# Turning q and k of one block and x of two blocks by transposing DMA instead of on TensorE

## The chip, the cores and the metric

The kernel runs on one core of a Trainium2 chip. The metric is the device time of one execution in microseconds (us). Three runs of the kernel before took 304.11, 304.75 and 304.83 us, so the median is 304.75 us. A profiled execution gives the trace that the text reads.

## The reference

Attention with a sliding window and a linear bias on the distance comes first, then a normalised two-layer network with a residual. B = 8 batches, H = 8 heads, S = 576 tokens, D = 64 per head, so 512 features per token and 2048 hidden ones.

```python
rel = pos[:, None] - pos[None, :]
bias = slopes[:, None, None] * (-np.abs(rel))            # one slope per head
mask = (rel >= 0) & (rel < 128)
scores = np.where(mask, q @ k^T / sqrt(D) + bias, -1e9)  # per batch and head
attn = softmax(scores)
x = heads of (attn @ v) side by side                     # B x 576 x 512
xn = (x - mean) / sqrt(var + 1e-6) * g_ln
out = x + relu(xn @ w_ch1) @ w_ch2                       # 512 -> 2048 -> 512
```

Inputs and output are float32; the kernel works on float16 tiles with float32 sums.

## The kernel before

**Blocks.** Two batches make a pair `p` (0 to 3). The tokens of a pair are cut into nine blocks of 128 rows: `blk` 0 to 7 are 128 tokens of one batch each (even ones of the first batch, odd ones of the second), and `blk` 8 (`T`) holds the last 64 tokens of both batches. All 36 blocks have a number n = 9 p + blk; "block 13" in the text is n = 13. Blocks are gathered in twelve groups for the network: groups 0 to 5 have two blocks each (group 3 has blocks 6 and 7), groups 6 to 11 have four.

**Loading.** `load_qk` and `load_v` issue DMAs on GpSimd's queue, which turn float32 into float16 on the way. q and k come for two blocks at once (index `i` = blk // 2; `i` = 4 is block 8 alone) and in two DMAs each, one for each batch. For `by_dma(p, i)` false, two neighbouring tokens go to one partition, so that one row of a DMA is 128 numbers (512 bytes of float32); for true, the tokens lie in their natural order and a row is 64 numbers (256 bytes). A GpSimd DMA waits, among other things, until the one eight before it has landed.

**Turning q and k.** The scores need q and k with the head's features on the partitions. `turn(p, i)` does that. Where `by_dma` is false, `transposed` makes transposes of 64x64 on TensorE (line 304), two times 16 for block 8, and copies take them out of PSUM on VectorE and ScalarE (line 348). Where it is true, `dma_start_transpose` is issued on SyncE's queue (line 322), one DMA for q and one for k and for each batch. `BY_DMA_TURN = (1, 0)` sets the border: pair 0 (blocks 0 to 8) is turned on TensorE, and everything from block 9 on by DMA.

**Turning x.** A block's attention output is `x`; the first network product needs it centred and with the features on the partitions, in the group's tile `xT`. For blocks below `BY_DMA` (8), `centre` writes the centred `xc` and `turn_x` makes four transposes on TensorE (line 638) and one copy out of PSUM (line 639). From block 8 on `normal` issues a transposing DMA on SyncE (line 548), but for the three blocks in `BY_PE`.

**Order.** `steps` is a list written out by hand, of scores, masks, values, turns and decays for blocks 4 to 9, and made by a loop from block 8 on. The main program runs the network's products (`mlp1`, line 815, the first product; `mlp2`, line 889, the second) and `weave_at` puts the next steps behind those products whose numbers it is given. TensorE, SyncE and GpSimd run in exactly the order in which the program issues. The scores are made by `attend` (line 442); the values by line 496. The scores of block n + 2 stand behind the values of block n.

SyncE's queue carries the stores of the results too (line 1052): two for each of the first blocks, each waiting until VectorE has made the result. A DMA on SyncE also waits until the one eight before it has landed. Raw q and k tiles and their turned forms have four buffers each, `xT` three, `xc` three.

Of the kernel before, what the change touches and what calls it, by code (L numbers as in the profile page):

```python
# [17 lines left out]
P = 128  # L18
# [8 lines left out]
FAST, HURRIED, DEFERRED, SETTLED, TURNED = 6, 11, 14, 15, 18  # L27

NV = 10
BY_DMA_TURN = (1, 0)  # L30
AHEAD, HELD = 8, (19, 23)

FIRST_GROUPS, FIRST = 2, 4
# [27 lines left out]
def kernel(  # L61
# [10 lines left out]
    nc = tc.nc  # L72
# [140 lines left out]
    def by_dma(p, i):  # L213
        return (p, i) >= BY_DMA_TURN

# [31 lines left out]
    order = [(p, blk) for p in range(NPAIR) for blk in range(NSLOT)]  # L247
# [137 lines left out]
    def psum(name, banks=None):  # L385


        if not ring:
            return ps_mm.tile([P, DM], FP32, tag="mm", name=name)
        t = (banks or ring)[0]  # L390
        if banks is None:
            ring.append(ring.pop(0))
        return t
# [127 lines left out]
    turned_x = {}  # L521

    centred = {}
# [33 lines left out]
    def inverse_roots(n=None):  # L557

        for left, m in roots[:]:
            if left <= 0 or m == n:  # L560
                roots.remove([left, m])
                inverse_root(m)
# [66 lines left out]
    def turn_x(g, at, p, blk, copy):  # L629
# [8 lines left out]
            nc.tensor.transpose(ps[:, kb, :], xc[:, kb * P : (kb + 1) * P], iden)  # L638
        copy(out=xT[:, :, at * P : (at + 1) * P], in_=ps)

    def variance(n):
        st = small.tile([P, nc.vector.BN_STATS_DIM], FP32, tag="st", name="st")
        nc.vector.bn_stats(out=st, in_=xs[order[n]])  # L643
        nc.vector.bn_aggr(out=moments[:, n, :], in_=st)
# [31 lines left out]
    members, home = [], {}  # L676
    for g, size in enumerate(GROUPS):
        n = sum(GROUPS[:g])
# [5 lines left out]
    def turn_step(n, *how):  # L684
        p, blk = order[n]
        return [(turn, p, blk // 2) + how]

    def scores_step(n):
        return [(scores,) + order[n]]

    def load_step(n):
        if n in HELD or n + AHEAD > count:
            return []
        if n < HELD[0]:
            return [(load_until, place[n + AHEAD])]
        return [(hold_loads, n), (load_until, place[min(n + AHEAD - 1, count - 1)])]
# [6 lines left out]
    def values_steps(n):  # L703
        p, blk = order[n]
        return [
            [(masks, p, blk), (values, p, blk, 0)],
            [(values, p, blk, 1), (centre, p, blk)] + load_step(n) * (n < BY_DMA),
        ]

    def x_step(n, copy=nc.vector.tensor_copy):  # L710
        return [(turn_x,) + home[n] + order[n] + (copy,)] if n < BY_DMA else []

    def variance_of(n):

        return [(variance, n)] + [(inv_std, n - 3, 4)] * (n % 4 == 3)

    def masks_of(n, *halves):
        return [(masks,) + order[n] + halves]

    def warm_step(n):  # L720
        return [[(warm, n)]]
# [8 lines left out]
    steps = warm_step(11) + [[(turn_first,)]] + warm_step(3)  # L730
# [17 lines left out]
    steps += [x_step(4) + masks_of(5)]  # L748
    steps += [values_steps(5)[0], turn_step(6, True), values_steps(5)[1]]
    steps += [scores_step(6) + [(decay, m_tail, 4)]]  # L750
    steps += [x_step(5) + masks_of(6) + turn_step(9), scores_step(7) + variance_of(4), values_steps(6)[0]]

    steps += [values_steps(6)[1], masks_of(7), x_step(6, nc.scalar.copy), variance_of(5)]
    steps += [*values_steps(7), x_step(7) + variance_of(6)]
    low, high = ([(decay, m_late, 5, range(h, h + 4))] for h in (0, 4))
    steps += [turn_step(8) + low + variance_of(7), scores_step(8) + turn_step(11)]
    steps += [[(scores_tail, 0)] + scores_step(9) + high + masks_of(8)]


# [38 lines left out]
    def advance_to(n):  # L798
        nonlocal done
        while done < min(n, len(steps)):  # L800
            for f, *args in steps[done]:
                f(*args)
            done += 1
# [4 lines left out]
    def hidden_tile(g):  # L808
        hidden[g] = hidden_pool.tile([P, NFB, 4 * P], FP16, tag="ht", name="ht")

    def ch1(g, fb, ps, cols):

        w = w1 if g < FIRST_GROUPS else w1g
        for kb in range(NKB):
            nc.tensor.matmul(  # L815
                ps[:, cols],
                w[:, kb, fb * P : (fb + 1) * P],
                turned_x[g][:, kb, cols],
                start=(kb == 0),
                stop=(kb == NKB - 1),  # L820
            )

    def relu(g, fb, ps, on_dve):
        cols = slice(0, len(members[g]) * P)
        out, ps = hidden[g][:, fb, cols], ps[:, cols]
        if on_dve:
            nc.vector.tensor_scalar(
                out=out, in0=ps, scalar1=0.0, scalar2=None, op0=ALU.max
            )
        else:  # L830
            nc.scalar.activation(out=out, in_=ps, func=AF.Relu)  # L831
# [35 lines left out]
    def mlp1(g, on_dve=()):  # L867
        cols = slice(0, len(members[g]) * P)
        hidden_tile(g)
        turn_about = chain(*zip(range(QF), range(QF, NFB)))  # L870
        for u, fb in enumerate(turn_about if g >= FAST else range(NFB)):
            ps = psum("ps_m1")
            ch1(g, fb, ps, cols)
            relu(g, fb, ps, u in on_dve)
            yield cols
            if g >= FAST and u == 10:
                for i in range(4):
                    combine_hidden(g, 0, i)

    def mlp2(g, parts=((0, NFB),)):  # L880

        ht = hidden[g]
        sums = {}
        for first, end in parts:
            for at, (p, blk) in enumerate(members[g]):
                if first == 0:
                    sums[at] = ps_mm.tile([P, DM], FP32, tag="mm", name="ps_m2")
                for fb in range(first, end):
                    nc.tensor.matmul(  # L889
                        sums[at],  # L890
                        ht[:, fb, at * P : (at + 1) * P],
                        w2[:, fb, :],
                        start=(fb == 0),
                        stop=(fb == NFB - 1),
                    )
                    if fb % 4 == 3 and fb < NFB - 1:
                        yield DM
                if end == NFB:
                    finish(p, blk, sums[at])
                    yield DM  # L900
# [10 lines left out]
    def combine_hidden(g, part, i):  # L911


        f = slice(part * QF // 2, (part + 1) * QF // 2)
        s1, s2, s3, s4 = (hidden_sum(g, j) for j in range(4))
        a11, a12 = (hidden_quarter(g, 0, j) for j in range(2))
        a21, a22 = (hidden_quarter(g, 1, j) for j in range(2))
        dst, a, b, op = (
            (s1, a21, a22, ALU.add),
            (s2, s1, a11, ALU.subtract),  # L920
            (s4, a12, s2, ALU.subtract),
            (s3, a11, a21, ALU.subtract),
        )[i]
        nc.vector.tensor_tensor(out=dst[:, f], in0=a[:, f], in1=b[:, f], op=op)
# [131 lines left out]
    def weave_at(units, *places, also=(), late=0):  # L1056
        nonlocal hold
        hold = late
        for u, _ in enumerate(units):
            for root in roots:  # L1060
                root[0] -= 1
            inverse_roots()
            advance_to(done + places.count(u))
            if u in also:
                next(combined, None)
# [12 lines left out]
    with tc.manual_schedule(engines={engine.PE, engine.SP, engine.Pool}):  # L1078
        with tc.manual_schedule(engines={engine.Activation, engine.DVE}):
            advance_to(first)  # L1080
            weave_at(mlp1_first(), 2, 3, 4, 8, 10, 12, 17, 24, 30, 34)
            weave_at(mlp2(0, [(fb, fb + 4) for fb in range(0, NFB, 4)]), 0, 1, 3, 4, 4, 5)
            weave_at(mlp2(1), 0, 1, 2, 3, 4, 6, 6)
            weave_at(mlp1(2), 0, 3, 5, 5, 6, 8, 13)
            weave_at(mlp2(2), 0, 2, 4, 6, 7)


            weave_at(mlp1(3, (9, 10, 11)), 8, 8, 12, 15, late=3)
            weave_at(mlp2(3), 0, 1, 1, 3, 4, 4, 6, 6)
            weave_at(mlp1(4, (11,)), 0, 4, 8, 10, 11, 14, also=(2, 12), late=3)  # L1090
            weave_at(mlp2(4), 0, 2, 2, 5, 5, 7, also=(1,))
            weave_at(mlp1(5, (0, 7)), 0, 4, 6, 8, 10, also=(3, 7, 11), late=3)
            weave_at(mlp2(5), 0, 1, 2, 4, 6, 7)
            ring += [ps_mm.tile([P, DM], FP32, tag="mm", name="ps_r") for _ in range(4)]
            for g in range(6, len(GROUPS)):
                weave_at(
                    mlp1(g), 0, 2, 5, 7, 8, 10, 13, 15, also=(1, 4) if g == 6 else ()
                )
                weave_at(fast_mlp2(g), 1, 3, 6, 7, 7, 10, 12, 13)
# [31 lines left out]
```

## Time and profile before

| | |
|---|---|
| median of 3 runs | 304.75 us |
| the profiled execution | 304.07 us |
| its span (first to last instruction) | 302.3 us |
| TensorE busy | 295.8 us, 98% of the span |
| VectorE busy | 216.8 us, 72% |
| ScalarE busy | 181.3 us, 60% |
| loads on GpSimd's queue (q0) | 108688 packets, 18.65 MB |
| DMAs on SyncE's queue (q1) | 49090 packets, 19.45 MB |
| granted TensorE clock | 0.994 |

The profiled execution's own time is 1.8 us more than its span. In the lines shown further down, PE is TensorE, DVE VectorE, ACT ScalarE, POOL GpSimd and SP SyncE; a q behind the name means the engine's queue, which issues and waits. L638 is line 638 of the kernel. The chain is the work that ended last, followed back from the last instruction. A busy share of DMA packets can be over 100%, since each of the 16 DMA engines has several packets under way at once.

### The profile page before, as it was taken

Reading aid. Unit: us, or ns where it says so; the run is one execution under the profiler, and the core shown is the slowest. Engines: PE = TensorE matmul, PEld = TensorE weight load, DVE = VectorE, ACT = ScalarE, POOL = GpSimd, SP = SyncE. Lnnn points to the kernel's source line nnn. Section 1 sums busy time; section 2 is a strip of 40 time slices with the busy share of each in tenths; the row PEclk is TensorE's granted clock in tenths of the full one; section 3 lists DMA queues with packets and bytes.
Section 4 is the critical chain, followed back from the end, with each engine's and each line's share of the span. In section 5 each row is a group of like instructions: output and inputs, shape, how many; then the busy total and the mean of one; then the engine's idle time right before and its main releaser. Section 6 shows DMA issues by size and latency. Waiting matters only on the chain.

```text
span 302.3 us, 8809 instructions
## 1 busy us (share of the span) xinstructions
PE 295.8 (98%) x3652; PEld 201.0 (66%) x3652; DVE 216.8 (72%) x518; ACT 181.3 (60%) x358; POOL 109.6 (36%) x145
## 2 busy tenths in 40 slices
PE   8999999999999999999999999999999999999994
PEld 2479755857768585557865786578657865784583
DVE  2589777867687797657976797679767976750463
ACT  5498776878769386485358536753685367306600
POOL 8936359843568333442173218312400000000001
PEclk9799999999999999999999999999999999999999
DMA  9999999999999999999899939999992051021004
GB/s 99 164 189 194 196 188 176 144 164 156 171 165 129 168 128 183 153 180 134 86 166 185 132 62 148 112 189 132 149 154 50 20 165 28 2 88 69 2 0 139
DMA packets 158042, 38.99 MB, mean 129 GB/s; under 512 B 147953, under 2 KB 153585, under 8 KB 158002
## 3 DMA queue, kind: packets, MB, share of 16 engines
q0 software_dynamic: 108688, 18.65, 88.3%
q1 hardware_dynamic: 49090, 19.45, 40.5%
q8 instruction: 28, 0.46, 0.7%
q10 hardware_dynamic: 224, 0.33, 0.3%
q14 instruction: 12, 0.10, 0.2%
HBM read 36.97 MB, written 9.44 MB: 154 GB/s over the span
## 4 chain that ended last, share of the span: by engine, by line
PE 95%; DMA 2%; DVE 1%; POOL 1%; issue 0%; DVEq 0%; POOLq 0%
PE ps_r L815 28%; PE ps_r L955 24%; PE ps_m L815 14%; PE ps_m L889 14%; PE ps_sc L442 6%; PE ps_r L496 3%; PE ps_pv L496 2%; DMA k<-in_k_dram 2%; PE ps_warm L286 1%; PE ps_tx L638 1%; DVE o L973 1%; PE ps_tr L304 1%; PE ps_sc L580 1%; POOL q L231 1%; PE ps_sc L304 0%; PE ps_sc L286 0%
## 5 line engine op out<-in xcount | busy, mean ns | idle before, releaser
L815 PEld LDWEIGHTS <-w1g 128*128 128x128 f16 x640 | 61.2, 98 | 47.1 <-issue 0.2
L815 PE MATMUL ps_r<-xT,w1g 128*128 128x512 f16 x384 | 84.8, 379 | 0.0
L451 ACT ACTIVATE probs<-ps_sc 128x1024 f16<-128x1024 f32 x56 | 54.2, 1025 | 35.4 <-PE ps_sc L442 35.4
L831 ACT ACTIVATE ht<-ps_r 128x512 f16<-128x512 f32 x96 | 55.7, 595 | 23.8 <-PE ps_r L815 23.8
L889 PE MATMUL ps_m<-w,ht 128*128 128x512 f16 x192 | 45.3, 380 | 0.0
L955 PE MATMUL ps_r<-w,ht 128*128 128x256 f16 x384 | 43.9, 273 | 0.0
L241 POOL DMA_DIRECT2D vx<-in_v_dram x40 | 34.0, 858 | 19.5 <-DMA k<-in_k_dram 3.9
L955 PEld LDWEIGHTS <-ht 128*128 128x128 f16 x384 | 37.2, 98 | 4.7
L831 ACT ACTIVATE ht<-ps_m 128x256 f16<-128x256 f32 x86 | 30.8, 391 | 5.3 <-PE ps_m L815 3.2
L228 POOL DMA_DIRECT2D k<-in_k_dram x30 | 25.3, 854 | 16.6 <-DMA q<-in_q_dram 14.0
L1048 POOL DMA_DIRECT2D out_dram<-o x2 | 1.1, 560 | 82.1 <-DVE o L973 82.1
L228 POOL DMA_DIRECT2D q<-in_q_dram x30 | 25.4, 853 | 14.9 <-DMA vx<-in_v_dram 13.8
L815 PE MATMUL ps_m<-xT,w1g 128*128 128x256 f16 x256 | 30.0, 273 | 0.0
L889 PEld LDWEIGHTS <-ht 128*128 128x128 f16 x192 | 17.3, 98 | 18.3
L462 DVE TENSOR_TENSOR probs<-probs,m 128x1024 f16<-128x1024 f16 x44 | 27.8, 672 | 0.1
L504 DVE RECIPROCAL rec<-ps_r 128x4 f32<-128x4 f32 x36 | 6.3, 174 | 28.1 <-PE ps_r L496 28.1
L643 DVE BATCH_NORM_STATS2 st<-x 128x6 f32<-128x512 f16 x36 | 24.8, 688 | 0.7
L955 PE MATMUL ps_r<-w,hs 128*128 128x256 f16 x192 | 21.9, 273 | 0.0
L973 DVE TENSOR_TENSOR o<-ps_r,o 128x512 f32<-128x512 f32 (+1 forms) x25 | 16.5, 664 | 5.6 <-PE ps_r L955 5.1
L496 PEld LDWEIGHTS <-probs 128*128 128x128 f16 x416 | 17.4, 97 | 4.5 <-DVE probs L462 0.3
L442 PE MATMUL ps_sc<-q,k 64*64 64x128 f16 (+1 forms) x1088 | 20.0, 210 | 0.3 <-DVE k L344 0.3
L955 PEld LDWEIGHTS <-hs 128*128 128x128 f16 x192 | 18.8, 98 | 2.2
(98 smaller groups left out, 360.7 us busy)
## 6 DMA issues: line engine op xcount, KB each, us to landing
out_dram<-o SPq DMA_DIRECT2D x22, 256.0 KB, 4.1
q<-in_q_dram POOLq DMA_DIRECT2D x32, 128.0 KB, 8.8
k<-in_k_dram POOLq DMA_DIRECT2D x32, 128.0 KB, 9.7
vx<-in_v_dram POOLq DMA_DIRECT2D x32, 128.0 KB, 11.7
w<-in_moe_w_ch_dram POOLq DMA_DIRECT2D x6, 512.0 KB, 10.4
out_dram<-o SPq DMA_DIRECT2D x24, 128.0 KB, 5.5
w<-in_moe_w_ch_dram POOLq DMA_DIRECT2D x4, 256.0 KB, 11.4
q<-in_q_dram POOLq DMA_DIRECT2D x8, 64.0 KB, 8.5
```

The lines of the kernel that those rows point to most:

```text
L228: nc.gpsimd.dma_start(out=dst, in_=rows.rearrange("h p d -> p h d"))
L241: nc.gpsimd.dma_start(out=vx[p0 : p0 + n, :, 0:D], in_=v[b, :, t0 : t0 + n, :].rearrange("h p d -> p h d"),)
L442: nc.tensor.matmul(at_q, kt[rows, hp, cols], of_q, start=True, stop=True,)
L451: nc.scalar.activation(out=dst.rearrange("p (n j) q -> p j n q", j=2), in_=ps.rearrange("p j n t q -> p j n (t q)"), func=AF.Exp, scale=in ...
L462: nc.vector.tensor_tensor(out=dst, in0=dst, in1=mask, op=ALU.mult)
L496: nc.tensor.matmul(ps[:, i, :], pr[:, h, t, :], vext[(p * NSLOT + o) % NV][:, h, :], start=(n == 0), stop=(n == len(terms) - 1),)
L643: nc.vector.bn_stats(out=st, in_=xs[order[n]])
L815: nc.tensor.matmul(ps[:, cols], w[:, kb, fb * P : (fb + 1) * P], turned_x[g][:, kb, cols], start=(kb == 0), stop=(kb == NKB - 1),)
L831: nc.scalar.activation(out=out, in_=ps, func=AF.Relu)
L889: nc.tensor.matmul(sums[at], ht[:, fb, at * P : (at + 1) * P], w2[:, fb, :], start=(fb == 0), stop=(fb == NFB - 1),)
L955: nc.tensor.matmul(banks[name][pair][:, pair, :], lhs[:, fb, pair * P : (pair + 1) * P], rhs[:, fb, :], start=(first and fb == 0 and (pair ...
L973: nc.vector.tensor_tensor(out=o[:, at, cols], in0=banks[name][at.start][:, at, :], in1=(x if to_x else o)[:, at, cols], op=ALU.add,)
```

## The change

The border of `BY_DMA_TURN` moves to (0, 4), so that block 8 is loaded in its natural order and its q and k are turned by two transposing DMAs. The turn of block 8 moves ahead of the turn of blocks 9 and 10 in the steps. `send_x` is new: it issues a transposing DMA for x of blocks 6 and 7, right behind their `centre`, in place of `turn_x` on TensorE. One step fewer is left, so `weave_at` for group 2's first product has one place less. The buffers are as before. In SyncE's queue the new DMAs stand as follows: stores of blocks 0 to 2, turn of 8, turn of 9/10, store of block 3, x of 6, x of 7, turn of 11/12.

```diff
@@ -27,7 +27,7 @@
 FAST, HURRIED, DEFERRED, SETTLED, TURNED = 6, 11, 14, 15, 18
 
 NV = 10
-BY_DMA_TURN = (1, 0)
+BY_DMA_TURN = (0, 4)
 AHEAD, HELD = 8, (19, 23)
 
 FIRST_GROUPS, FIRST = 2, 4
@@ -638,6 +638,11 @@
             nc.tensor.transpose(ps[:, kb, :], xc[:, kb * P : (kb + 1) * P], iden)
         copy(out=xT[:, :, at * P : (at + 1) * P], in_=ps)
 
+    def send_x(g, at, p, blk):
+
+        xT = turned_x[g][:, :, at * P : (at + 1) * P]
+        nc.sync.dma_start_transpose(out=xT, in_=centred.pop((p, blk)))
+
     def variance(n):
         st = small.tile([P, nc.vector.BN_STATS_DIM], FP32, tag="st", name="st")
         nc.vector.bn_stats(out=st, in_=xs[order[n]])
@@ -710,6 +715,9 @@
     def x_step(n, copy=nc.vector.tensor_copy):
         return [(turn_x,) + home[n] + order[n] + (copy,)] if n < BY_DMA else []
 
+    def send_step(n):
+        return [(send_x,) + home[n] + order[n]]
+
     def variance_of(n):
 
         return [(variance, n)] + [(inv_std, n - 3, 4)] * (n % 4 == 3)
@@ -748,12 +756,12 @@
     steps += [x_step(4) + masks_of(5)]
     steps += [values_steps(5)[0], turn_step(6, True), values_steps(5)[1]]
     steps += [scores_step(6) + [(decay, m_tail, 4)]]
-    steps += [x_step(5) + masks_of(6) + turn_step(9), scores_step(7) + variance_of(4), values_steps(6)[0]]
-
-    steps += [values_steps(6)[1], masks_of(7), x_step(6, nc.scalar.copy), variance_of(5)]
-    steps += [*values_steps(7), x_step(7) + variance_of(6)]
+    steps += [x_step(5) + masks_of(6) + turn_step(8) + turn_step(9), scores_step(7) + variance_of(4), values_steps(6)[0]]
+
+    steps += [values_steps(6)[1] + send_step(6), masks_of(7), variance_of(5)]
+    steps += [values_steps(7)[0], values_steps(7)[1] + send_step(7), variance_of(6)]
     low, high = ([(decay, m_late, 5, range(h, h + 4))] for h in (0, 4))
-    steps += [turn_step(8) + low + variance_of(7), scores_step(8) + turn_step(11)]
+    steps += [low + variance_of(7), scores_step(8) + turn_step(11)]
     steps += [[(scores_tail, 0)] + scores_step(9) + high + masks_of(8)]
 
 
@@ -1081,7 +1089,7 @@
             weave_at(mlp1_first(), 2, 3, 4, 8, 10, 12, 17, 24, 30, 34)
             weave_at(mlp2(0, [(fb, fb + 4) for fb in range(0, NFB, 4)]), 0, 1, 3, 4, 4, 5)
             weave_at(mlp2(1), 0, 1, 2, 3, 4, 6, 6)
-            weave_at(mlp1(2), 0, 3, 5, 5, 6, 8, 13)
+            weave_at(mlp1(2), 0, 3, 5, 6, 8, 13)
             weave_at(mlp2(2), 0, 2, 4, 6, 7)
```

## The prediction

> **What bounds the kernel now.** First the head of the page and its chain: TensorE works for nearly the whole span, and the chain that ended last is TensorE's own.
>
> ```profile
> span 302.3 us, 8809 instructions
> PE 295.8 (98%) x3652; PEld 201.0 (66%) x3652; DVE 216.8 (72%) x518; ACT 181.3 (60%) x358; POOL 109.6 (36%) x145
> ...
> PE 95%; DMA 2%; DVE 1%; POOL 1%; issue 0%; DVEq 0%; POOLq 0%
> ```
>
> So TensorE time taken out is time won, as long as nothing that TensorE needs comes late. Next the chain in order of time (start, duration, what) around the three turns that the change touches.
>
> ```profile
> 50.74 1.73 PE ps_m L889 x8
> ...
> 57.11 0.22 PE ps_tx L638 x4
> ...
> 61.31 0.22 PE ps_tx L638 x4
> ...
> 63.27 0.62 PE ps_tr L304 x32
> 63.90 1.83 PE ps_m L889 x8
> ...
> 72.27 7.09 PE ps_m L815 x64
> ```
>
> 57.11 and 61.31 turn x of blocks 6 and 7, 63.27 turns q and k of block 8, and 72.27 is the first product of group 3, which reads the turned x of 6 and 7. No idle time stands between the pieces. Third, SyncE's queue over the same time (start, duration, what), since the turns go there.
>
> ```profile
> 50.13 1.11 SPq L1052 DMA_DIRECT2D out_dram<-o  x2
> 52.58 2.69 SPq L322 DMA_TRANSPOSE q<-q  x2
> 55.44 2.68 SPq L322 DMA_TRANSPOSE k<-k  x2
> 58.22 2.31 SPq L1052 DMA_DIRECT2D out_dram<-o  x2
> 61.11 2.62 SPq L322 DMA_TRANSPOSE q<-q  x2
> 64.10 3.26 SPq L322 DMA_TRANSPOSE k<-k  x2
> ...
> 76.37 3.33 SPq L322 DMA_TRANSPOSE k<-k  x2
> ```
>
> These are the turns of block pairs 9/10 (52.58), 11/12 (61.11) and, last line, 13/14. One transposing DMA holds the queue for some 1.34 us. In the DMA view of narrow stretches the issues at 64.10 and 76.37 land after:
>
> ```profile
> k<-k SPq DMA_TRANSPOSE x1, 9.0
> k<-k SPq DMA_TRANSPOSE x1, 7.9
> ```
>
> Last, what transposes do to the loads. The DMA view of 75.3 to 76.3 us, in which no transpose moves, and then of 66.5 to 69.5 us, in which they do; q0 carries GpSimd's loads, q1 SyncE's DMAs (packets, MB, share):
>
> ```profile
> q0 software_dynamic: 1195, 0.15, 236.4%
> q1 hardware_dynamic: 9, 0.01, 2.5%
> ```
> ```profile
> q0 software_dynamic: 1525, 0.19, 98.3%
> q1 hardware_dynamic: 1139, 0.28, 71.8%
> ```
>
> Alone, the loads run at 1195 packets a us; beside transposes at 508, with 380 transposing packets. And the rate from 55 to 73.3 us, in 40 slices of 0.46 us, in which eight transposes ran:
>
> ```profile
> GB/s 166 173 170 90 43 126 153 187 142 151 66 14 10 156 153 153 159 152 151 158 158 256 315 198 155 158 160 150 159 160 147 190 149 81 8 53 154 155 151 155
> ```
>
> Three times (slices of 43, of 14 and 10, and of 8) all queues all but stop, for 1.0 to 1.5 us. From 35 to 50 us, without transposes, no slice is under 108. So this stretch of DMA is full, though TensorE does not yet wait for it.
>
> **What goes.** On TensorE 8 + 32 transposes and nothing else: its order is otherwise the same. From the chain: 0.22 + 0.22 + 0.62, and the eight products after the turn of block 8 take 1.83 us instead of 1.73, so 0.10 more: 1.16 us, all on the path. The four copies out of PSUM (0.42 and 0.73 us on VectorE, 0.58 and 0.73 on ScalarE) go too; I count them at nothing, as both engines wait for TensorE there. Four PSUM tiles less can only free waits, of which the chain shows none. That alone is 304.07 - 1.16 = 302.91 us against the profiled execution, which lies 0.68 us under the median of 304.75; so 303.6 as a median.
>
> **What comes.** Four transposing DMAs in SyncE's queue: q and k of block 8 ahead of turn 9/10, x of 6 and 7 behind the store of block 3 and ahead of turn 11/12. And the four loads of block 8 fetch rows of 256 bytes instead of 512: by the code 512 packets each instead of 256. GpSimd takes 0.68 us instead of 0.58 to issue one (rows of the same form later on): 0.4 us in all, covered, as GpSimd then waits until 45.31 for another reason.
>
> *Block 8.* Its loads are issued by 43.8 and land 5.3 to 6.3 us later, by 50.1 at the latest, so its two transposes can go at 51.3, once the stores of block 2 are out. Landing 9.0 us after issue, k is there at 61.6; scores of block 8 stand at 65.7 - 1.06 = 64.6. Covered by 3 us. Behind them turn 9/10 issues about 1.5 us later than now: its first k lands at about 66, and its scores stand at 67.9 - 1.16 = 66.7. Covered, but only just.
>
> *x of 6 and 7.* The centred x is ready (60.5 for block 7). On the queue: 51.3 + 6 x 1.34 + 1.1 for two stores = 60.5 for x6, 61.9 for x7. Needed: 72.2 - 1.16 = 71.0. If the issue sets the pace, x7 lands 7.3 to 9.0 us later (the neighbouring rows), at 69.2 to 70.9: in time. If the transposing queue sets the pace, x7 is the eighth of a row of eight transposes with two stores among them, as the second k of 11/12 is now: issued at 66.1 and, with the 9.0 us of the k before it (its own landing is not recorded), there at about 75.1. The row begins 1.3 us sooner, so 73.8: 2.8 us late. The queue looks full in the 66.5 row, so I take the middle, 0.9 us late; ends 0 and 2.8.
>
> *Loads behind them.* Each added transpose has 512 packets, 1.35 us at 380 a us, in which the loads lose (1195 - 508) x 1.35 = 925 packets or 0.77 us; four make 3.1. The added load packets are 1024, at most 0.9 us; I take 0.6, as their neighbours land in 5 to 6 us and the queue was not yet full. Three stops for eight transposes make one and a half for four; I take one of 1.1 us (ends 0 and 1.8). Together the loads of block pair 13/14 land 4.8 us later (3.1 to 5.8). Nothing shortens that on the way: GpSimd waits for landed DMAs before it issues more (14.0 and 13.8 us of such waits at its k and q loads). Turn 13/14 starts now when its loads land; its first k, issued at 76.37, lands at 84.3 and is used by the scores of block 13 at 87.9. Slack 3.7, less the 1.16 that TensorE comes sooner: 2.5. So 4.8 makes TensorE wait 2.3 us (0.6 to 3.3). What it waited for x7 counts within this, since it moves the scores back too. What is late next would be turn 15/16 (first k landing at 96.3 for scores at 100.6, 4.3 us of slack, and 2.3 more after the wait): covered.
>
> Sum: -1.16 + 2.3 = +1.14 us, 304.07 + 1.14 = 305.2 for the profiled execution, 305.9 as a median.
>
> **A rule against this change.** The trace turns a 128x512 tile on TensorE in 0.22 us and by DMA in 7.3 to 9.0 us here. The Trainium skill, "VectorE: DVE Perf Modes", section "The three transpose paths" (and its rules for authors), prefers TensorE wherever PSUM will do as a destination, with 390 ns for one 128x128 turn there against 1309 ns by DMA. The direction agrees; the size does not, as four turns in 0.22 us are 55 ns apart. By the page's 390 ns, as an estimate, the eight turns of x alone would free 3.1 us instead of 0.44, and the sum would be a gain of 1.5 us.
>
> **Rivals.**
> *All lands in time.* The issue paces x7, and the transposes mostly use slots that the loads leave. For it: the 7.3 us rows, and 3.7 us of slack at 13. Between 146 and 152 us, with no loads, a transpose lands in 2.4 us and its 512 packets take about 0.64 us (1993 packets, 41.9% of 6 us). Were that the whole cost, four would be 2.6 us, 0.1 over the slack before stops. Against it: the halved load rate. It decides as long as x7 lands by 71.0 and the loads of 13/14 come less than 2.5 us later. Time: 303.6, not slower but 1.16 us faster. The Trainium skill, "Advanced Engine Details and Errata", section "X-Bar Transpose (TRN2)", has transposes as fast as plain DMAs at 350 to 400 GB/s, an estimate of 0.35 us for one; that would also lead here, but the slices above show 150 to 160 GB/s.
> *Only x7 is late,* and the loads recover by 73 us. TensorE waits 0.3 to 2 us at the start of group 3's first product: 303.9 to 305.6, middle 304.7.
> *Worse than forecast.* Two or more added stops, or turn 9/10 late as well: waits of 3.5 to 5 us, 307.1 to 308.6. For it: three stops in one row of eight. Against it: the loads run without stops from 75 to 79 us, and turn 15/16 has its slack.
> *The change doesn't do what it says:* TensorE's order shows the transposes gone, so this is out.
>
> **Numbers.** Forecast (turn 13/14 late) 0.42; all in time 0.30; x7 alone 0.21; worse 0.07. The forecast's own range is 304.2 to 306.9, from 0.6 and 3.3 us of waiting. The range from 303.4 (the in-time case, with 0.2 for scatter) to 307.2 leaves out some 0.1 to 0.2. About 0.3%, 0.9 us, is what a measurement can tell from no change: faster by more is the in-time case, 0.30; the x7 case and the low end of the forecast lie within, 0.23; slower 0.47.
>
> **What would show it.** Right: TensorE's chain has gaps released by DMA near 71 us (group 3's first product) and near 87 us (scores of block 13), with 1 to 3 us between them; the loads of 13/14 land about 5 us later; outside, the pieces of the chain keep their lengths. Wrong: no such gaps and a span 1.1 us shorter; or a first gap at the scores of block 9, or lateness that is still there after 110 us.

## The result, and the profile after

The changed kernel takes 307.02 us (median of 8 runs, 305.26 to 309.39) against 304.37 us (median of 8 runs, 303.01 to 304.83): a ratio of 1.0095, 95% interval 1.0072 to 1.0118. It is 2.65 us slower, where 1.14 us were forecast. The profiled execution took 306.27 us. The ratios here and below leave out runs that took over 1.5% more than the fastest of their kernel.

First the head of the page and its chain by engine, for the kernel after.

```profile
span 304.5 us, 8738 instructions
PE 295.5 (97%) x3612; PEld 200.3 (66%) x3612; DVE 215.9 (71%) x516; ACT 180.6 (59%) x356; POOL 110.2 (36%) x145
...
PE 89%; DMA 4%; DVE 3%; issue 1%; POOL 1%; SPq 1%; ACT 1%; DVEq 0%; POOLq 0%
```

The 40 transposes are gone (3612 matrix instructions instead of 3652), and yet TensorE is busy for 295.5 us instead of 295.8. So something else has become longer on it. The chain's share of TensorE fell from 95% to 89%: it now leaves TensorE somewhere. Where, the chain in order of time tells (start, duration, what):

```profile
64.41 8.61 DMA xT<-xc
73.02 0.05 issue
73.07 8.83 PE ps_m L823 x64
...
90.54 0.47 PE ps_sc L442 x16
```

The transposing DMA of x of block 7 is issued at 64.41 and lands at 73.02; group 3's first product starts the moment it does. Two things are new. TensorE waited: its view of waits has one long entry.

```profile
PE ps_m L823 <- DMA xT<-xc: 2.5, 1, 2.5
...
PE ps_sc L442 <- DMA k<-k: 0.4, 1, 0.4
```

And the product itself is longer: its 64 instructions took 7.09 us before and take 8.83 us now. Tables of single microseconds show why (columns: stretch and its length, busy time and count of PE, PEld, DVE, ACT and POOL, granted clock, DMA share, GB/s):

```profile
72.00:73.00 1.00, 0.00 (x0) 0.00 (x0) 0.97 (x4) 0.00 (x0) 0.00 (x0) 1.00 1.23 123
73.00:74.00 1.00, 0.93 (x5) 0.71 (x6) 0.54 (x1) 0.00 (x0) 0.14 (x1) 0.59 1.81 155
74.00:75.00 1.00, 1.00 (x7) 0.73 (x5) 0.00 (x0) 0.47 (x2) 0.74 (x1) 0.50 1.89 153
75.00:76.00 1.00, 1.00 (x7) 0.69 (x6) 0.00 (x0) 0.53 (x2) 0.00 (x0) 0.50 1.99 153
76.00:77.00 1.00, 1.00 (x8) 0.78 (x7) 0.00 (x0) 0.53 (x2) 0.70 (x1) 0.70 1.66 155
77.00:78.00 1.00, 1.00 (x11) 0.90 (x10) 0.00 (x0) 0.77 (x3) 0.47 (x2) 1.00 1.61 154
```

The third figure from the end is the granted clock. It is still 1.00 while TensorE stands idle, falls to half when work starts again, and is back at 1.00 by 77. In the records the half clock lasts 3.41 us, in which 16 products come 213 ns apart instead of 109 ns: 16 x 104 ns = 1.7 us. The lateness of one transfer therefore cost twice, 2.46 us of waiting and 1.74 us of slow work behind it.

The Trainium skill, "TensorE: Matmul & The Clock Gate", has the clock fall back after about 3 us without work (section "Why this matters for your kernels") and states the limit as some 3.4 us (section "HAM oscillation — how this bites in real kernels"). The trace does not agree with that limit: 2.46 us were enough here.

SyncE's queue (start, duration, what) shows how x came to be that late:

```profile
50.87 1.35 SPq L322 DMA_TRANSPOSE q<-q  x1
52.40 1.29 SPq L322 DMA_TRANSPOSE k<-k  x1
53.85 2.87 SPq L322 DMA_TRANSPOSE q<-q  x2
56.89 4.71 SPq L322 DMA_TRANSPOSE k<-k  x2
61.71 1.21 SPq L1060 DMA_DIRECT2D out_dram<-o  x2
63.02 2.65 SPq L644 DMA_TRANSPOSE xT<-xc  x2
65.83 3.24 SPq L322 DMA_TRANSPOSE q<-q  x2
69.23 3.57 SPq L322 DMA_TRANSPOSE k<-k  x2
```

50.87 and 52.40 are q and k of block 8, and the turn of 9/10 follows 1.3 to 1.5 us later than before. But the two k of 9/10 hold the queue for 4.71 us instead of 2.68, and x7 (x of block 7; x6 is that of block 6) goes out at 64.41, not at 61.9 as worked out. The rates from 55 to 73.3 us, in 40 slices of 0.46 us, show something else in both places:

```profile
GB/s 141 142 117 137 154 100 144 88 9 9 73 151 145 129 136 147 159 140 152 153 151 155 154 156 143 153 256 256 254 156 160 150 155 193 142 102 8 56 159 150
```

All queues stop twice. The slices of 9 (58.7 to 59.6 us) lie within the 4.71 us for which the two k hold the queue, and the slice of 8 (71.5 to 71.9 us) within the 8.61 us for which x7 is under way. So about 1 us at the issue and somewhat less in flight go with stops, which the prediction had counted for the loads alone. How late x7 would have been without them is not shown.

DMA is as full as before; the DMA view of 66.5 to 69.5 us (packets, MB, share):

```profile
q0 software_dynamic: 1654, 0.21, 107.8%
q1 hardware_dynamic: 716, 0.40, 63.6%
```

In the same stretch SyncE's DMAs moved 1139 packets and 0.28 MB before. The 716 packets are fewer but have more bytes, since stores of results, in larger packets, are among them; so the two counts can't be compared as a rate of transposing. What the prediction expected at 87 us is not there: the first k of block 13 lands at 87.08, and its scores stand at 90.54. Its loads, as far as their landing is recorded, land 2.6 to 4.2 us later than before, but TensorE is later too.

How the profiled executions add up: ahead of the first removed turn, the changed kernel's chain is already 1.08 us sooner (49.66 for 50.74, the same eight products); nothing in the change does that, and the kernel of the first experiment, the same up to there, has 50.85. So -1.08 of scatter, -1.16 for the turns, +0.4 at the scores of block 9, +2.46 and +1.74 at group 3: +2.36, against +2.2 in the spans.

### The profile page after: what moved, and what is told of

The parts are those of the page before. It is cut to its first block, busy times and chain, and to the rows that moved or that the text cites. A ratio compares the mean times of both kernels' runs of the same rounds, so it can differ in the third digit from the quotient of the medians.

```text
span 304.5 us, 8738 instructions
## 1 busy us (share of the span) xinstructions
PE 295.5 (97%) x3612; PEld 200.3 (66%) x3612; DVE 215.9 (71%) x516; ACT 180.6 (59%) x356; POOL 110.2 (36%) x145
## 4 chain that ended last, share of the span: by engine, by line
PE 89%; DMA 4%; DVE 3%; issue 1%; POOL 1%; SPq 1%; ACT 1%; DVEq 0%; POOLq 0%
PE ps_r L823 28%; PE ps_r L963 24%; PE ps_m L823 13%; PE ps_m L897 11%; PE ps_sc L442 5%; DMA xT<-xc 3%; PE ps_r L496 3%; PE ps_pv L496 2%; DMA k<-in_k_dram 1%; PE ps_tx L638 1%; DVE o L981 1%; PE ps_sc L580 1%; POOL q L231 0%; PE ps_sc L304 0%; SPq L644 0%
## 5 line engine op out<-in xcount | busy, mean ns | idle before, releaser
L823 PEld LDWEIGHTS <-w1g 128*128 128x128 f16 x640 | 62.1, 99 | 50.6 <-DMA xT<-xc 2.6
L823 PE MATMUL ps_m<-xT,w1g 128*128 128x256 f16 x256 | 31.4, 282 | 2.5 <-DMA xT<-xc 2.5
L228 POOL DMA_DIRECT2D q<-in_q_dram x32 | 26.7, 839 | 19.0 <-DMA vx<-in_v_dram 16.4
L228 POOL DMA_DIRECT2D k<-in_k_dram x32 | 26.6, 838 | 14.7 <-DMA q<-in_q_dram 13.6
```

What stands on the lines that cost most here:

```text
L228: nc.gpsimd.dma_start(out=dst, in_=rows.rearrange("h p d -> p h d"))
L823: nc.tensor.matmul(ps[:, cols], w[:, kb, fb * P : (fb + 1) * P], turned_x[g][:, kb, cols], start=(kb == 0), stop=(kb == NKB - 1),)
```

## The experiments

The theories: (A) x7 comes late because the two halves of the change stand in one queue, and idle time then halves the clock; against it, that x by DMA is late by itself (B), that block 8's q and k upset the turns behind them (C), and, for what paces the queue, the loads (D) or the transposes themselves (E).

**x alone.** Turn x of 6 and 7 by DMA, keep block 8 on TensorE in its old place. Against the kernel after:

```diff
-BY_DMA_TURN = (0, 4)
+BY_DMA_TURN = (1, 0)
-    steps += [x_step(5) + masks_of(6) + turn_step(8) + turn_step(9), scores_step(7) + variance_of(4), values_steps(6)[0]]
+    steps += [x_step(5) + masks_of(6) + turn_step(9), scores_step(7) + variance_of(4), values_steps(6)[0]]
-    steps += [low + variance_of(7), scores_step(8) + turn_step(11)]
+    steps += [turn_step(8) + low + variance_of(7), scores_step(8) + turn_step(11)]
```

> x of blocks 6 and 7 turned by DMA; q and k of block 8 stay on TensorE, in their old place. Theory A (x7 is late because two transposes of block 8 stand ahead of it in the queue, and the idle time then halves the clock): x7 is the sixth of its row and not the eighth and lands about 70 us, 1.5 us or more before its product; no wait at group 3, the saving of 0.44 us is kept, about 304.0 us against 304.4. Theory B (a transposing DMA is too slow for x7 wherever it stands): a wait of 2 us or more at group 3 and a half clock behind it, 307 us.

Measured: 303.66 us, ratio 0.9984 (0.9964 to 1.0003). x7 was issued at 61.80 and landed at 69.54. The chain at group 3:

```profile
72.06 7.09 PE ps_m L823 x64
```

No wait and full clock; x7 was there 2.5 us early, so x by DMA is not late by itself: B is out. Against this kernel the change issues x7 2.61 us later, it takes 0.88 us longer (with a stop of the queues in it, where x7 here had none), and TensorE is ready 1.45 us sooner (1.19 of it the scatter named above, 49.66 for 50.85): 4.94 us, which uses up the 2.5 us and leaves the 2.46 us of waiting.

**q and k of block 8 alone.** The kernel before with that half of the change.

```diff
-BY_DMA_TURN = (1, 0)
+BY_DMA_TURN = (0, 4)
-    steps += [x_step(5) + masks_of(6) + turn_step(9), scores_step(7) + variance_of(4), values_steps(6)[0]]
+    steps += [x_step(5) + masks_of(6) + turn_step(8) + turn_step(9), scores_step(7) + variance_of(4), values_steps(6)[0]]
-    steps += [turn_step(8) + low + variance_of(7), scores_step(8) + turn_step(11)]
+    steps += [low + variance_of(7), scores_step(8) + turn_step(11)]
```

> q and k of block 8 turned by DMA ahead of 9/10; x of 6 and 7 stay on TensorE. Theory A: nothing is waited for at group 3; 0.72 us saved, less a wait of some 0.4 us at the scores of block 9: 303.9 to 304.2. Theory C (the step of the prediction: the added transposes make the loads and the turn of 13/14 late): half of the added transposes make the loads 2.7 us late against 3.0 of slack, 303.7 to 304.7, with the first wait at the scores of block 13.

Measured: 303.35 us, ratio 0.9981 (0.9957 to 1.0005). Group 3's product stands at 71.56 for 7.09 us, without a wait, and the scores of block 13 do not wait either, so nothing of C is seen here. Each half alone is no slower than before; the medians are 0.47 and 0.78 us under that of the kernel before in the same runs, together 1.25, close to the 1.16 us counted. Both at once should then have won 1.25 and lost 2.65: 3.9 us, give or take about 1 us by the three intervals, come of the two meeting.

**A filler in the idle time.** The kernel after, with twelve products on constants where TensorE would wait for x7.

```diff
             weave_at(mlp2(2), 0, 2, 4, 6, 7)
+            warm(12)
```

> The changed kernel with twelve idle products of 128x512 (2.6 us) on TensorE between the scores of block 10 and the first product of group 3, so that it works through the wait. Theory A: the wait for x7 ends when it did, but the clock stays at 1.0 and the 16 products at half clock go, 1.7 us: about 305.3 us against 307.0. If the slow products had another cause than the idle time, nothing is won: 307.0 or more.

Measured: 306.14 us, ratio 1.0063 (1.0037 to 1.0090). The filler in TensorE's timeline, and then lines of its chain:

```profile
71.17 2.76 PE L286 MATMUL ps_warm<-ones 128*128 128x512 f16 x12
```
```profile
65.75 8.60 DMA xT<-xc
...
74.49 7.15 PE ps_m L823 x64
```

x7 came at 74.4 in this execution, later still than in the kernel after, and TensorE waited all the same; but the products behind it ran at full clock, 7.15 us instead of 8.83. The mean granted clock of the other executions says the same. A stretch of 3.41 us at half clock in 302 us makes 0.994; seven of the eight runs of the kernel after have 0.992 to 0.994, and the eighth, at 1.0, is the fastest (305.26 us). With the filler none of twelve is below 0.997. (The kernel before has 0.996 or more in all 87 runs made beside the experiments; the 0.994 of its profiled execution was another, early stretch.) That the half clock is caused by the idle time is thereby shown. Its 1.7 us are read from the trace; the times alone do not settle them, since the two ratios' intervals overlap.

**Block 8's turn earlier.** The kernel after, with q and k of block 8 ahead of the store of block 2 in SyncE's queue.

```diff
-    steps += [values_steps(5)[0], turn_step(6, True), values_steps(5)[1]]
+    steps += [values_steps(5)[0], turn_step(6, True), values_steps(5)[1] + turn_step(8)]
-    steps += [x_step(5) + masks_of(6) + turn_step(8) + turn_step(9), scores_step(7) + variance_of(4), values_steps(6)[0]]
+    steps += [x_step(5) + masks_of(6) + turn_step(9), scores_step(7) + variance_of(4), values_steps(6)[0]]
```

> The changed kernel with the turn of block 8 ahead of the store of block 2 in SyncE's queue, where the queue sits idle until that store's result is there. All four added transposes stay. Theory A: x7 is the sixth transpose behind the store and lands at 70 us, as needed: no wait or less than 1 us, 303.2 to 304.5 us. Theory C: with x7 in time the turn of 13/14 is late instead, waits of 1 to 2.3 us at the scores of block 13 and a half clock behind: 305 to 307. Theory B: 307.

Measured: 304.45 us, ratio 1.0013 (0.9984 to 1.0043). x7 is issued at 62.92, 1.49 us sooner, and group 3 starts without a DMA wait. TensorE's timeline:

```profile
71.28 7.16 PE L823 MATMUL ps_m<-xT,w1g 128*128 128x256 f16 x64
...
87.84 0.51 PE L442 MATMUL ps_sc<-q,k 64*64 64x128 f16 x28 [0.58 <-DMA k<-k]
```

Here the forecast's own step comes out: with group 3 in time, the scores of block 13 wait for their k, for 0.58 us instead of the 2.3 worked out, and without a loss of clock. Their loads, as far as recorded, land 3.3 to 4.4 us later than in the kernel before, where the prediction had 4.8. One of twelve runs still has a clock of 0.994, and it is the slowest, 307.28 us.

**Fewer loads, first try.** The kernel after without the loads of v of blocks 10 to 16.

```diff
+        if 10 <= p * NSLOT + blk <= 16:
+            return
```

> The changed kernel without the loads of v for blocks 10 to 16 (seven loads of 128 KB less; the values of those blocks are then made from old numbers). Theory D (the transposing queue is slow because each of its packets shares the DMA engines with a packet of the loads): with fewer loads under way between 51 and 75 us a transpose moves in less than 1.3 us, x7 lands 2 us or more sooner than in the changed kernel (about 70 to 71 us), no wait at group 3, 303 to 304 us. Theory E (the queue or its issue is slow by itself, 1.3 us and more for each transpose): x7 lands at about 73 as before, the wait of some 2.5 us stays, 306 to 307 us.

Measured: 304.85 us, ratio 1.0010 (0.9976 to 1.0044). The profiled execution still waited:

```profile
72.92 8.83 PE L825 MATMUL ps_m<-xT,w1g 128*128 128x256 f16 x64 [2.41 <-DMA xT<-xc]
```

GpSimd issued its next loads into the places left free, so its queue stayed full (5829 packets of loads from 66 to 78 us, 5950 in the kernel after). The ten runs fall in two: six of 302.95 to 305.47 us with a clock of 0.998 or more, and four of 306.20 to 307.51 at 0.993 or 0.994, of which the last is not in the ratio. Something had changed for the better, but the trace can't say what, as it is of the late kind.

**The kernel after once more.** A single run, for a second trace.

> The changed kernel once more, for a second trace of the same wait. Theory A: again a wait for x7 before the first product of group 3, of 1.5 to 4 us, and half clock for some 3 us behind it; the scatter of the kernel's times comes from the length of this wait. Otherwise the wait lies elsewhere in this trace.

Measured: 307.74 us. TensorE's timeline:

```profile
74.47 8.83 PE L823 MATMUL ps_m<-xT,w1g 128*128 128x256 f16 x64 [2.54 <-DMA xT<-xc]
```

The product starts 1.4 us later than in the first trace, but the wait (2.54 us for 2.46) and the 8.83 us are as before: no accident of one trace. A rival remains. In all four traces in which x7 was late (the kernel after twice, the filler, the first try with fewer loads) a stop of all queues falls into the time for which x7 is under way; with x alone, and with block 8's turn earlier, x7 lands before the next stop. A later issue thus also let x7 run into a stop, and no run separates the two.

**Fewer loads, second try.** The kernel after with q and k of blocks 13 to 17 set to zero by GpSimd, and one head of eight of v of blocks 10 to 17 loaded.

```diff
+            if p == 1 and i > 1:
+                nc.gpsimd.memset(t, 0.0)
+                return
+        few = 1 if 10 <= p * NSLOT + blk <= 17 else H
-                out=vx[p0 : p0 + n, :, 0:D],
+                out=vx[p0 : p0 + n, 0:few, 0:D],
```

> The changed kernel with q and k of blocks 13 to 17 set to zero on GpSimd instead of loaded, and of v of blocks 10 to 17 one head of eight loaded; so the load queue is nearly empty from about 60 us, and stays so until the loads of block 18. Theory D (the transposing queue is slow because its packets share the DMA engines with the loads): from 60 us on a transpose moves in 0.9 us or less, x7 lands 3 us or more sooner after its issue than the 8.6 us of the changed kernel, so by about 69 us; no wait at group 3, full clock: 303.0 to 303.6 us. Theory E (queue or issue slow by itself): 8 us from issue to landing and the wait of 2.5 us as before, 306 to 307 us.

Measured: 303.21 us, ratio 0.9975 (0.9952 to 0.9997). Nine of the ten runs have a clock of 0.998 or more; the tenth, 307.17 us at 0.994, is not in the ratio, and no trace of it tells why. First the DMA view of 66.5 to 69.5 us, then TensorE's timeline:

```profile
q1 hardware_dynamic: 2230, 0.65, 132.2%
q0 software_dynamic: 144, 0.02, 8.9%
```
```profile
70.76 7.16 PE L827 MATMUL ps_m<-xT,w1g 128*128 128x256 f16 x64
...
87.50 0.51 PE L446 MATMUL ps_sc<-q,k 64*64 64x128 f16 x28 [0.75 <-DMA k<-k]
```

With nearly no loads beside them, SyncE's DMAs move 0.65 MB in 3 us instead of 0.40 (2230 packets instead of 716, but of another mix). x6 lands 5.47 us after its issue, not 7.30; x7 is issued at 64.57, even a little later than in the kernel after, and is there by 70.76, so at most 6.2 us instead of 8.61, though a stop falls into its flight here too. TensorE does not wait. So D holds for the flight, and E as the whole cause is out: sharing with the loads makes a transpose some 2 us slower. That is less than the 3 us that D foretold, and the issue of x7 did not come sooner. The Trainium skill, "DMA: Bandwidth & Descriptors", section "Queues, rings and completion order", has each DMA engine serve its queues in turn, packet by packet; the trace agrees, as the packets of the one queue go up when the other has few, though other ways of sharing would show the same.

The scores of block 13 wait 0.75 us although their q and k were not loaded at all. The chain has the first k of block 13:

```profile
77.68 9.77 DMA k<-k
```

It is issued at 77.68, behind stores and other turns, and takes 9.77 us to land. By then the loads of block 18 and on are under way (4140 packets of loads from 77.6 to 87.5 us, 2276 packets of SyncE's), and the queues stop once, near 80 us. So this wait does not tell the queue from the loads.

**Which half to keep.** Two more: block 8's early turn by DMA with x of 7 alone on TensorE (of 6 by DMA), and with both x on TensorE, that is, the kernel before with

```diff
-BY_DMA_TURN = (1, 0)
+BY_DMA_TURN = (0, 4)
-    steps += [values_steps(5)[0], turn_step(6, True), values_steps(5)[1]]
+    steps += [values_steps(5)[0], turn_step(6, True), values_steps(5)[1] + turn_step(8)]
-    steps += [turn_step(8) + low + variance_of(7), scores_step(8) + turn_step(11)]
+    steps += [low + variance_of(7), scores_step(8) + turn_step(11)]
```

The edit of the former, against the kernel with block 8's turn earlier:

```diff
-    steps += [values_steps(7)[0], values_steps(7)[1] + send_step(7), variance_of(6)]
+    steps += [values_steps(7)[0], values_steps(7)[1], x_step(7) + variance_of(6)]
```

> As the kernel with the early turn of block 8, but x of block 7 on TensorE; x of block 6 by DMA. Three added transposes. Saving 0.94 us. If the turn of 13/14 is late in proportion to the added transposes, it comes 0.8 us sooner than with four and its wait of 0.6 us is gone: about 303.4 us. Otherwise a wait of 0.3 to 0.6 at the scores of block 13, 303.9.

Measured: 304.76 us, ratio 1.0003 (0.9981 to 1.0025). Group 3 is in time, but TensorE waits 1.43 us for a load of v near 20 us (the kernel with block 8 alone by DMA waits 1.20 us there) and 1.36 us for k at 118 us. Why there, is open. One of the twelve runs, 308.73 us at a clock of 0.992, is not in the ratio.

> q and k of block 8 by DMA, ahead of the store of block 2; x of 6 and 7 on TensorE. If the waits are what the change lost, this keeps its 0.72 us of TensorE time and two added transposes: about 303.6 us against 304.3, no wait on a DMA after 60 us. If turn 13/14 is already late with two added transposes, a wait of up to 0.5 us at the scores of block 13 and 304.1.

Measured: 303.81 us, ratio 0.9981 (0.9961 to 1.0001); its profiled execution has no wait of TensorE for a DMA. Run again:

> The early turn of block 8 by DMA with x of 6 and 7 on TensorE, measured a second time, to tell whether it beats the kernel before: 0.72 us of TensorE time saved and no wait, 0.9976; with the first measurement (0.9981) the upper end should come under 1. If scatter in the loads eats it, 0.999 to 1.001.

Measured: 303.42 us, ratio 0.9976 (0.9954 to 0.9997). In its profiled execution TensorE waits for a DMA for 0.5 us or less at a time. This version is 0.2% faster than before, at the edge of what was measured, and by the two ratios 1.2% faster than the kernel after (0.9976 / 1.0095 = 0.988).

## Why the prediction was right or wrong, step by step

- **What goes, 1.16 us of TensorE:** right. The two halves alone bring 0.47 and 0.78 us in the medians, where 0.44 and 0.72 were counted.
- **Block 8 covered, turn 9/10 only just:** block 8 was; the scores of block 9 waited 0.4 us.
- **x of 6 and 7, "0.9 us late; ends 0 and 2.8":** this is the step that failed. The wait was 2.46 us, and it stood in the place of the one forecast at block 13. The flight (issue to landing), 8.61 us, lay within the 7.3 to 9.0. The issue was mis-sized: the sum 51.3 + 6 x 1.34 + 1.1 gave each transpose 1.34 us of the queue and nothing for delays, and the two k of 9/10 held it for 4.71 us, so that x7 went out at 64.41 instead of 61.9. A stop of all queues, about 1 us, lies in those 4.71 us; what made the rest of the 2.03 us by which they exceed the 2.68 of before stays open. The end at which the queue sets the pace gave 73.8 for x7, and it came at 73.02. The row of 66.5 us, which showed the queue full, spoke for that end, and the middle was taken.
- **What TensorE does after a wait:** the missing term, put at nothing without a reason. The sum had every product at the length it had before; 1.74 us of half clock came on top of the wait.
- **Turn 13/14 late, 2.3 us:** did not happen. The loads were 2.6 to 4.2 us later instead of 4.8 (the stop of 1.1 us taken for them was not added: two stops from 55 to 73.3 us, three before), and TensorE, later by the wait and by the half clock, came to the scores of block 13 after their k. The text had said that waiting for x7 counts within this wait; it did not see that it could be longer than it. With group 3 in time the wait is there, 0.58 us.
- **The rivals:** "only x7 is late" named the right place, with 0.3 to 2 us of waiting; "worse" had the right size, by a mechanism that was not seen.
- **The rule against this change:** not settled. The three measurements with block 8 by DMA and x on TensorE have the lowest ratios of those that do the whole computation (0.9976 to 0.9981), but x alone by DMA, at 0.9984, cannot be told from them.

So the direction came out right by another wait than the one forecast, which is in part luck.

## What to carry to other kernels

A transfer that a dense stretch of TensorE waits for costs its lateness and then the slow clock: where a gap of some 2.4 us or more can open, add the 1.7 us, or have something run in it. Two edits that are each harmless can share a queue, so add up the queue with both, with room for delays in it, and when one row shows it full, take the end at which it sets the pace. Off-loading from a bound engine pays where the result has slack: block 8's q and k had it, x had 2.5 us by itself and none beside them.

## What the runs showed of the hardware that was not expected

- Idle times of TensorE of 2.41, 2.46 and 2.54 us each brought 3.41 us at half clock; idle times of 0.58, 1.36 and 1.43 us brought none. Where between 1.43 and 2.41 us the limit lies was not tried. In the traces with a half clock the changes of the granted clock lie whole multiples of 3.41 us apart (in the kernel after at 4.92, 73.19 and 76.60 us; 68.27 is 20 x 3.41), and each of the three long gaps lies between two such marks; so it may matter where a gap begins, which was not tried either.
- The same transposing DMA of 128x512 takes 2.4 us from issue to landing alone, 5.47 us beside other transposes and some 6.5 to 10 us beside loads as well.
- All DMA queues stop together for up to 1.5 us now and then, with loads or nearly without: the rates from 55 to 73.3 us in 40 slices, of the kernel with few loads.

```profile
GB/s 122 115 146 132 155 129 74 72 8 9 90 154 152 153 156 151 152 151 160 163 192 103 202 150 248 355 253 281 233 252 181 0 10 8 116 170 31 135 157 0
```

The slices of 8 and 9 and of 0, 10 and 8 are such stops; when the second came, few loads were under way, so loads are not needed for one. What makes them stays open.
